# A fused top-k attention and SwiGLU kernel: each unit's product with V two turns after its top-k instead of four, with the exponential first in ScalarE's turn

## The chip, the cores and the metric

The kernel runs on one core of a Trainium2 chip. The metric is device microseconds of one execution. The kernel before takes 1840.27 us, the median of 3 runs (1840.24 to 1840.27).

A core has five engines, each with its own instruction stream that it works off in order: TensorE (PE in the profile; PEld is its weight load), VectorE (DVE), ScalarE (ACT), GpSimd (POOL) and SyncE (SP, which issues most DMAs here). An instruction that waits holds up everything behind it on its own engine, and nothing on the others until they need its result.

## The reference

Attention with a mask: per batch and head (8 batches, 8 heads, 576 tokens, head dimension 64), all but the 32 largest scores of a row are left out of the softmax. The result of the 8 heads side by side, 4608 tokens by 512, goes through a SwiGLU block with 1536 hidden columns. All is float32; the three weights arrive as float64.

```
scores = scale * np.matmul(q, k.transpose(0, 1, 3, 2))
kth = np.partition(scores, -top_k, axis=-1)[..., -top_k:-top_k + 1]
scores = np.where(scores >= kth, scores, -1000000000.0)
attn = np.exp(scores - np.max(scores, axis=-1, keepdims=True))
attn = attn / (np.sum(attn, axis=-1, keepdims=True) + 1e-09)
x = np.matmul(attn, v)        # then (B,H,S,D) -> (B*S, H*D)
g = x @ w_gate
out = (g / (1 + np.exp(-g)) * (x @ w_val)) @ w_out
```

## The kernel before

**Units and turns.** Attention is cut into 160 units (L281): a batch, a block of query rows, and a pair of heads. A batch has 20 units: 16 full ones (128 rows of each of two heads) and then 4 half ones (the last 64 rows of both heads, stacked into one tile of 128 partitions). The main loop (L718 to L774) has one turn per unit, and in turn n each engine works on a different unit:

- VectorE: `select(n)` (L326), the top-k of unit n: per head four MAX8 (L339) and three MATCH_REPLACE8 (L343), then a compare-and-multiply (L349) that leaves a penalty in `e`. Between these it does the rounding of the float64 weights (L124, L130) in the first turns, and one reciprocal (L382).
- TensorE: `scores(n+1)` (L304, L318), the transposes of a normalized unit (`turn`, L397), its product with V (`values`, L417, L426), transposes of new k and q (`prep`, L265, L273), and pieces of the feed-forward block.
- GpSimd: `penalize(n-1)` (L353): a bias (L359) and the sum e + scores (L361).
- ScalarE: `weigh(n-1)` (L364), the exponential with row sum (L370) and a small sum (L375); the scaling by the reciprocal (`normalize`, L385); and every copy out of PSUM: scores to `sc` (L309, L323), transposes to `et` (L398), attention output to `xT` (L441), k and q (L268 to L278), the feed-forward products (L505 to L507, L512) and sums (L593, L600, L624, L636).

The order on each engine is the order in which the Python code emits the instructions: the last lines (L781 to L794) chain every engine's instructions in that order. So where a call stands in the loop decides who waits for whom.

**How long a unit takes in turns.** Unit u has its top-k in turn u and its exponential in turn u+1. Its reciprocal and scaling come in turn u+2 (`over`, L721 and L724), its transposes at the head of turn u+3 (`TURN = 3`), and its product with V at the head of turn u+4 (`VALUES = 4`). The loop has four more turns than units. The tile `e` has 4 buffers.

**Feed-forward.** The attention output collects in `xT` blocks of 256 tokens by 512. When all of a block's units are in (`done`, L659), `feed(kb)` (L466) may run: 18 blocks. Per block, six times (s = 0 to 5) a gate product and a value product into a PSUM tile `f` (3 buffers). A gate product is followed by three ScalarE instructions (tanh, half, plus one) and a GpSimd product h * half; a value product by a ScalarE copy and a GpSimd product h * val. The tiles `half_g` and `val` share three buffers, tag "gv". Then comes the product with w_out, for block 0 directly (L526), for the others in seven partial products ("quarters", L566) whose operands and results GpSimd adds and subtracts (L573, L581, L586, L614, L552). `feed` is a generator; each step ("piece", cost 1) is 4 matmul instructions of 128x256, and 3 of a quarter's six matmuls cost 0.75. In the trace a matmul instruction on float32 shows as two records, so a piece is 8 records and a product (gate or value of one s) 16.

**How pieces are placed.** A turn's share of pieces is `share(n)` (L679): 6.4 per full unit (3.2 per half), less what the unit work of that turn costs TensorE. The turn's credit is spent at fixed places of the turn, `pieces(2)`, `pieces(1)`, `pieces(1)`, `pieces(6)`; in the last four units it is 8.

**Delayed work of ScalarE and GpSimd.** What follows a feed-forward product is not emitted at once, but put on the lists `on_act` and `on_pool`, which `flush` empties: both in `piece()` when they hold more than one entry, both at the turn's head, `on_act` after `pieces(2)`, `on_pool` after the scaling. A quarter adds flushes of its own. At the head of a turn the order is: `on_act`, `penalize(n-1)`, `on_pool`, transposes of n-3, product with V of n-4, scores of n+1 on TensorE, exponential of n-1, scores of n+1 out of PSUM.

The PSUM tiles of scores, transposes, av and kqps share 5 buffers (`ps_t`); `sc` has 2.

The lines of the code:

## Time and profile before

| | |
|---|---|
| median of 3 runs | 1840.27 us |
| the profiled execution, its own time | 1837.67 us |
| its span, first to last instruction | 1835.9 us |
| mean granted TensorE clock | 0.965 |
| PE busy | 1705.2 us (93%) |
| PEld busy | 1406.3 us (77%) |
| DVE busy | 1618.9 us (88%) |
| ACT busy | 1202.6 us (66%) |
| POOL busy | 1013.0 us (55%) |
| e + scores on GpSimd (L361), one of a full unit | 2.64 us |
| h * half and h * val on GpSimd (L508, L513), one | 1.28 us, 1.30 us |
| exponential of one head on ScalarE (L370) | 0.78 us |
| last threshold instruction of unit 159 (L349) ends at | 1737.5 us |

Busy time is the union of an engine's instructions, so waits are what is left. The chain that ended last is 83% PE. The 1.8 us between span and own time lie around the program; the median of the runs is 2.6 us above the profiled execution. In what follows a "turn n" of the trace runs from the end of unit n-1's last threshold instruction on VectorE (L349) to the end of unit n's.

### The profile page before, as it was taken

What the parts mean: (1) busy time and instruction counts of PE and PEld (TensorE: products, weight loads), DVE (VectorE), ACT (ScalarE), POOL (GpSimd) and SP (SyncE); (2) the same over time, 40 slices, a digit from 0 to 9 for tenths busy, and PEclk for the clock granted to TensorE, in tenths of its full rate; (3) what the DMA queues carried; (4) which work ended last, traced back from release to release, by engine and by line L of the source; (5) the groups of instructions that cost most, each with busy time, mean ns of one, the idle gap of its engine ahead of it and who ended that gap; (6) DMA issues with size and microseconds to landing.
All of it is one profiled execution on the core that took longest, in us unless ns stands there. A gap on an engine that the chain in (4) does not pass through costs nothing.

```text
span 1835.9 us, 30517 instructions
## 1 busy us (share of the span) xinstructions
PE 1705.2 (93%) x10756; PEld 1406.3 (77%) x10756; DVE 1618.9 (88%) x3405; ACT 1202.6 (66%) x2943; POOL 1013.0 (55%) x932
## 2 busy tenths in 40 slices
PE   3448999999999989999999999999999999999998
PEld 2336758777888878887888878888788878888887
DVE  7999999999999889997999989998999989998300
ACT  5667766677666667666767676767776766675431
POOL 3556746645555545655464646564556554646444
PEclk7668999999999999999999999999999999999999
DMA  7332121000200021000300012000300011000000
GB/s 189 98 84 91 59 66 26 12 1 21 73 1 12 2 66 27 12 1 15 73 19 1 12 42 52 1 12 2 74 19 12 1 36 32 1 12 12 1 13 12
DMA packets 109145, 59.65 MB, mean 32 GB/s; under 512 B 88512, under 2 KB 96704, under 8 KB 108992
## 3 DMA queue, kind: packets, MB, share of 16 engines
q1 hardware_dynamic: 107936, 57.44, 12.1%
q8 instruction: 85, 1.39, 0.3%
q14 instruction: 68, 0.56, 0.1%
q10 hardware_dynamic: 1056, 0.26, 0.1%
HBM read 48.23 MB, written 9.44 MB: 31 GB/s over the span
## 4 chain that ended last, share of the span: by engine, by line
PE 83%; DVE 3%; POOL 2%; ACT 2%; issue 2%; POOLq 0%; ACTq 0%
PE f L480 39%; PE x_ps L566 9%; PE av L426 8%; PE etps L397 7%; PE s L318 7%; PE y_ps L566 7%; PE s L304 2%; PE av L417 1%; DVE m L339 1%; PE kqps L273 1%; DVE rest L343 1%; PE o_ps L526 1%; POOL e L361 1%; POOL p L552 0%; ACT e L370 0%
## 5 line engine op out<-in xcount | busy, mean ns | idle before, releaser
L339 DVE MAX8 m<-rest 128x8 f32<-128x576 f32 x864 | 619.3, 758 | 2.2
L343 DVE MATCH_REPLACE8 rest<-m,rest 128x576 f32<-128x576 f32 x576 | 427.1, 754 | 0.0
L361 POOL TENSOR_TENSOR e<-e,sc 128x1152 f32<-128x1152 f32 (+1 forms) x160 | 382.7, 2392 | 79.7 <-DVE e L349 61.0
L480 PE MATMUL f<-xT,wg 128*128 128x256 f32 x1728 | 401.6, 382 | 0.0
L480 PE MATMUL f<-xT,wv 128*128 128x256 f32 x1728 | 400.4, 382 | 0.0
L480 PEld LDWEIGHTS f<-xT,wg 128*128 128x128 f32 x1728 | 323.0, 190 | 62.6 <-issue 21.0
L480 PEld LDWEIGHTS f<-xT,wv 128*128 128x128 f32 x1728 | 325.3, 190 | 59.5 <-issue 16.6
L508 POOL TENSOR_TENSOR h<-h,half_g 128x512 f32<-128x512 f32 x108 | 138.1, 1279 | 295.6 <-ACT h L507 295.1
L339 DVE MAX8 m<-sc 128x8 f32<-128x576 f32 x288 | 206.4, 757 | 105.8 <-ACT sc L309 57.9
L370 ACT ACTIVATE e<-e,bias 128x576 f32<-128x576 f32 x288 | 222.1, 777 | 89.5 <-POOL e L361 89.5
L397 PE MATMUL etps<-ident,e 128*128 128x128 f32 (+1 forms) x1312 | 184.0, 285 | 96.9 <-POOL size L120 40.8
L398 ACT COPY et<-etps 128x512 f32<-128x512 f32 (+1 forms) x448 | 184.4, 484 | 124.6 <-PE etps L397 123.6
L397 PEld LDWEIGHTS etps<-ident,e 128*128 128x128 f32 (+1 forms) x1312 | 158.3, 146 | 124.3 <-POOL size L120 43.3
L513 POOL TENSOR_TENSOR h<-h,val 128x512 f32<-128x512 f32 x108 | 139.9, 1295 | 186.0 <-ACT val L512 185.8
L385 ACT ACTIVATE e<-e,tot 128x576 f32<-128x576 f32 x288 | 211.9, 789 | 7.0 <-DVE tot L382 6.7
L343 DVE MATCH_REPLACE8 rest<-m,sc 128x576 f32<-128x576 f32 x288 | 213.0, 750 | 0.0
L318 PE MATMUL s<-kqT 64*128 64x288 f32 x1024 | 171.6, 445 | 5.8 <-ACT kqT L278 3.6
L349 DVE TENSOR_SCALAR e<-sc,m 128x576 f32<-128x576 f32 x288 | 171.8, 640 | 3.4
L426 PE MATMUL av<-et,v 128*64 128x128 f32 (+1 forms) x2560 | 172.4, 280 | 0.0
L323 ACT COPY sc<-s 128x288 f32<-128x288 f32 x512 | 163.9, 402 | 1.8 <-PE s L318 1.7
L426 PEld LDWEIGHTS av<-et,v 128*64 128x64 f32 x2560 | 135.7, 144 | 22.7 <-issue 6.6
L505 ACT ACTIVATE h<-f 128x512 f32<-128x512 f32 x108 | 65.3, 605 | 130.9 <-PE f L480 130.9
(71 smaller groups left out, 2010.0 us busy)
## 6 DMA issues: line engine op xcount, KB each, us to landing
v<-in_v_dram SPq DMA_DIRECT2D x32, 256.0 KB, 3.0
kq_in<-in_k_dram SPq DMA_DIRECT2D x63, 128.0 KB, 3.0
kq_in<-in_q_dram SPq DMA_DIRECT2D x63, 128.0 KB, 3.0
w<-in_moe_w_gate_dram SPq DMA_DIRECT2D x12, 512.0 KB, 3.7
w<-in_moe_w_val_dram SPq DMA_DIRECT2D x12, 512.0 KB, 3.8
w<-in_moe_w_out_dram SPq DMA_DIRECT2D x12, 512.0 KB, 3.6
out_dram<-o SPq DMA_DIRECT2D x40, 128.0 KB, 2.4
out_dram<-o SPq DMA_DIRECT2D x16, 256.0 KB, 2.4
```

What stands on the lines that cost most here:

```text
L318: nc.tensor.matmul(ps[:, 0:half], slab[d, q0 : q0 + P], slab[d, k0 : k0 + half])
L339: nc.vector.max(m[:, t, 8 * r : 8 * r + 8], cur[:, hs])
L343: nc.vector.match_replace(rest[:, hs], m[:, t, 8 * r : 8 * r + 8], cur[:, hs], LOWEST)
L349: nc.vector.tensor_scalar(e[:, hs], sc[:, hs], m[:, t, TOP_K - 1 : TOP_K], FAR, ALU.is_lt, ALU.mult)
L361: nc.gpsimd.tensor_tensor(e[:, every], e[:, every], sc[:, every], ALU.add)
L370: nc.scalar.activation(e[:, hs], e[:, hs], AF.Exp, bias=bias[:, t : t + 1], scale=scale, accum_out=tot[:, t : t + 1],)
L385: nc.scalar.mul(e[:, hs], e[:, hs], tot[:, t : t + 1])
L397: nc.tensor.transpose(ps[0:kl, c * P : (c + 1) * P], e[:, k0 : k0 + kl], ident[:])
L398: nc.scalar.copy(et[0:kl, c0 : c0 + cn, :], ps[0:kl, 0 : cn * P].rearrange("p (c j) -> p c j", c=cn),)
L426: nc.tensor.matmul(av[hh * R : (hh + 1) * R, 0:ql], v_last[:, hh, :] if c == J else vt[:, hh, c, :], moving, start=last and c == 0, stop=c ...
L480: nc.tensor.matmul(ps[:, i, :], w[:, kc, m * P : (m + 1) * P], x[:, kc, :], start=(kc == 0), stop=(kc == KC - 1),)
L566: nc.tensor.matmul(ps, lhsT, T[i][m], start=m == 0, stop=m == MQ - 1)
```

## The change

In the new order a unit has its exponential, reciprocal, scaling and transposes all in the turn after its top-k (the transposes late in it, in front of `pieces(6)`), and its product with V in the turn after that, behind the scores. The loop has two more turns than units, and `share` counts the unit work accordingly. At a turn's head ScalarE first gets the exponential, then the delayed feed-forward work, then the copies of the scores. GpSimd's delayed products are no longer emitted in `piece()` nor after the scaling, but at the head of the turn behind the sum e + scores. Where more than two wait when a "gv" buffer is wanted, the oldest are emitted then (the new function `gv`); the flushes of the quarters and at the start of a block remain.

```diff
+    def gv(name):
+        while len(on_pool) > 2:
+            on_pool.pop(0)()
+        return ffn.tile([P, 2, BLK], FP32, tag="gv", name=name, bufs=3)
...
-                half = ffn.tile([P, 2, BLK], FP32, tag="gv", name="half_g", bufs=3)
+                half = gv("half_g")
...
-                val = ffn.tile([P, 2, BLK], FP32, tag="gv", name="val", bufs=3)
+                val = gv("val")
...
-        if len(on_pool) > 1:
-            flush(on_pool)
...
-        for m, cost in ((n + 1, 0.7), (n - TURN, 0.6), (n - VALUES, 0.7)):
+        for m, cost in ((n + 1, 0.7), (n - 1, 0.6), (n - 2, 0.7)):
...
-    TURN, VALUES = 3, 4
-    for n in range(NU + VALUES):
+    for n in range(NU + 2):
...
-        over[n - 1] = normalize(n - 1) if 0 <= n - 1 < NU else no
-        norm = over.pop(n - 2, no)
+        norm = normalize(n - 1) if 0 <= n - 1 < NU else no
...
-        flush(on_act)
         if 0 <= n - 1 < NU:
             penalize(n - 1)
         flush(on_pool)
-        if 0 <= n - TURN < NU:
-            run(turn(n - TURN))
-        if n >= VALUES:
-            finish_unit(n - VALUES)
-        next(nxt, None)
         early[0]()
         if 0 <= n - 1 < NU:
             weigh(n - 1)
+        flush(on_act)
         run(nxt)
+        if n >= 2:
+            finish_unit(n - 2)
...
         dve(1)
         dve(1)
-        next(norm, None)
-        run(norm)
-        flush(on_pool)
         next(ahead, None)
         pieces(1)
         next(ahead, None)
         dve(1)
+        run(norm)
         pieces(1)
         dve(2)
         run(topk)
+        if 0 <= n - 1 < NU:
+            run(turn(n - 1))
         pieces(6)
```

More of the change, by code (lines that the diff above doesn't have):

```diff
@@ L714 @@
     no = iter(())
-    over = {}
-    TURN, VALUES = 3, 4
     due = [2.0]
-    for n in range(NU + VALUES):
+    for n in range(NU + 2):
         nh = n_heads(units[n][1]) if n < NU else 1
         topk = select(n) if n < NU else no
-        over[n - 1] = normalize(n - 1) if 0 <= n - 1 < NU else no
         nxt = scores(n + 1) if n + 1 < NU else no
         ahead = fetch(n + 2) if n + 2 < NU else no
-        norm = over.pop(n - 2, no)
+        norm = normalize(n - 1) if 0 <= n - 1 < NU else no
         def dve(k, beside=True):
```

## The prediction, written before the changed kernel ran

> **What bounds the kernel now.** I read the page's slices first, then windows of single stretches, then the timeline by engine around one change of feed-forward block, and last the waits. The slices say who is full where:

> ```profile
> PE   3448999999999989999999999999999999999998
> DVE  7999999999999889997999989998999989998300
> ACT  5667766677666667666767676767776766675431
> PEclk7668999999999999999999999999999999999999
> ```

> For four slices (184 us) DVE is full and PE is not; after that PE is full to the end, DVE has gaps, and in the last two slices DVE is done while PE works off feed-forward blocks. ACT is never full. So the time is PE's work plus PE's waits, and the waits lie at the start. The windows (columns: length, then busy time of PE, PEld, DVE, ACT, POOL, then PE's granted clock):

> ```profile
> 130.00:144.00 14.00, 7.40 (x45) 5.61 (x43) 13.50 (x30) 10.08 (x23) 8.20 (x9) 0.70 0.32 96
> 144.00:158.00 14.00, 6.81 (x41) 5.68 (x42) 14.00 (x29) 9.21 (x21) 7.81 (x7) 0.76 0.30 94
> 354.00:365.00 11.00, 6.74 (x42) 5.33 (x43) 10.99 (x25) 8.54 (x22) 4.24 (x4) 0.79 0.13 48
> 640.00:656.00 16.00, 11.38 (x80) 8.42 (x79) 6.60 (x13) 8.45 (x23) 9.39 (x12) 0.89 0.02 5
> 1012.00:1472.00 460.00, 456.72 (x2956) 380.22 (x2956) 436.84 (x919) 315.82 (x783) 258.42 (x234) 1.00 0.09 23
> ```

> The first two are turns 9 and 10, where PE idles half the time: no block is complete yet. The third is turn 29, idle again because block 2 is not complete. The fourth is one of the few stalls later on, and the last shows the rule: 99% busy. That this busy time is real I take from the spacing of weight loads: 16 of one product start at 1734.81 us and the next 16 at 1738.27 us, 0.216 us each, and it is the same all through the full stretch. One piece (8 records) is 1.73 us.

> The PE timeline at the start of block 2 gives the rest of the prices:

> ```profile
> 374.44 1.24 PE L318 MATMUL s<-kqT 64*128 64x288 f32 x8
> 375.62 3.72 PE L480 MATMUL f<-xT,wg 128*128 128x256 f32 x16
> ...
> 384.35 1.15 PE L397 MATMUL etps<-ident,e 128*128 128x128 f32 x9
> 385.33 0.39 PE L417 MATMUL av<-et,vlast 128*128 128x128 f32 x2
> 385.65 1.09 PE L426 MATMUL av<-et,v 128*64 128x128 f32 x16
> 386.68 1.24 PE L318 MATMUL s<-kqT 64*128 64x288 f32 x8
> 387.85 0.48 PE L480 MATMUL f<-xT,wg 128*128 128x256 f32 x1
> ```

> From start to start: transposes 0.98 us, product with V 1.35, scores 1.17, together 3.5 us a full unit. With the planner's 6.4 - 2.0 = 4.4 pieces, a full turn is 3.5 + 4.4 x 1.73 = 11.1 us of PE, against 10.56 us of DVE in the turns where DVE does not wait (thresholds of units 32 to 35, L349). PE is the longer one by 0.5 us, so it falls behind DVE until DVE waits for scores; that is the state of the full stretch.

> **Step 1, the feed-forward block starts two turns earlier.** In the new program order the first feed-forward matmul stands in turn 9 (24 matmul instructions) instead of turn 11, into PE idle time of 14.0 - 7.40 + 14.0 - 6.81 = 13.8 us. But the work then runs dry again: block 2 needs units up to 27, so PE waits for it in turn 31 now and in turn 29 then. It is cleaner to compare these two restarts. Now block 2 starts at 375.62 us. Then, turn 29 begins where DVE has finished unit 28, at 354.2 us (I take DVE's pace there as unchanged: it is full, and its instructions are the same in number). From there a chain is new, because xT's copy stands behind the exponential and the scores on ACT. The ACT timeline:

> ```profile
> 378.28 0.78 ACT L370 ACTIVATE e<-e,bias 128x576 f32<-128x576 f32 x1 [3.40 <-POOL e L361]
> ...
> 379.94 0.30 ACT L375 ACTIVATE tot<-tot,eps 128x2 f32<-128x2 f32 x1
> ```

> POOL's sum ends 2.8 us after DVE's threshold, the exponential takes 1.96 us (378.28 to 380.24), four copies of scores 1.28, two of xT 0.33: block 2 starts at 354.2 + 6.4 = 360.6. At 375.62 PE has by now done two scores and one transpose group more than then (2 x 1.17 + 0.98 = 3.3 us). PE comes out of a wait there, so 3.4 us run at half clock (the 640 window, after a wait of 4.6 us, has clock 0.89 over 16 us, about 3.5 us at half): 1.7 us lost. Gain: 375.6 - 360.6 - 3.3 - 1.7 = **10.0 us**. Bounds: 4 (VectorE delayed 3 us in turns 17 to 28, the clock lost twice) to 14.8 (xT's copy as early as now).

> **Step 2, the full stretch.** The units' work, the pieces and the copies are the same instructions; what changes is what PE can wait for. At the transposes (L397) PE now needs an e that was scaled in the same turn. With PE level with DVE, PE gets there at 1.17 + 1.35 + 4 x 1.73 = 9.4 us into the turn. On the other side: sum at 2.8, exponential to 4.7, scores and xT to 6.4, reciprocal after 10 of the 14 top-k instructions (about 6.8), then two scalings (1.47 us): 8.3. But ACT's feed-forward work stands ahead of the scalings: a gate is 0.605 + 0.601 + 0.641 = 1.85 us by its rows. With one gate it is 9.7 and the first scaling is out at 9.0, no wait; with a second gate left over from the turn before it is 10.8 for the first scaling, a wait of 1.4 us. If PE lags 2 us or more there is none, and PE lags by itself, 0.5 us more every full turn. Behind a waiting transpose stand up to six pieces and the next scores; behind the waiting exponential, ACT's copies, which PE needs for PSUM (3 buffers of f: two products waiting and one more to fill, 3.5 us, after 2.5 us of unit work; ACT is back by then). GpSimd's products, held back to the head, put one or two more of them (1.28 us each) between the first subtraction of a quarter and its addition: the third quarter would find its operand up to 2 us late at lag 0, and in time at lag 2.

> On the other side stand the stalls of now: 17 us of PE idle between 376 us and the tail. They come from POOL being stuck in feed-forward work when the sum is due:

> ```profile
> ACT e L370 <- POOL e L361: 89.5, 42, 4.9
> ```

> With the products at the head only, most of that cause goes; the quarters' own additions stay in front of the sum. Bounds for the stretch: -17 us (all stalls gone) to +103 full turns x 1.4 us = +144. I take **0**, near the low end, as PE has the longer turn and so the lag.

> **Step 3, the tail.** After the last scores there are 44.25 pieces against 52 now: these 7.75 pieces are the same two turns as step 1, not a second gain. Block 16 runs out sooner, so the last chain is open: exponential of unit 159 (behind the et copies of 158), reciprocal, output copy, scaling, transposes, et, V, xT. By the rows above: about 3.4 us of PE idle where now there are 1.0 + 0.4. **+2 us.**

> **Costed at nothing:** loads of v two turns earlier (DMA share 0.09); fewer or later flushes (order, no instruction); the smaller number of turns (empty ones). One weight piece moved ahead by a turn on DVE around turn 12, 1.2 us, made good in the next.

> **Sum.** 1835.9 - 10.0 + 0 + 2 = 1828 us of span; the own time 1.8 us more; the median of the runs 2.6 us above that: **1832 us**, 0.45% faster.

> [...]

> **Rivals.**
> - *The wait at the transposes (slower).* PE doesn't build up the lag, because DVE now waits for the exponential (L382 stands in DVE's stream, and its input hangs on ACT behind PE's last transposes): et copies 0.7, exponential 2.0 and a gate 1.85 must fit before 6.8, so DVE waits once the lag is above about 2.3 to 4 us. If it settles below 2, PE waits in most full turns. The gain is gone at 8 / 103 = 0.08 us a full turn. At 0.3 us: 1832 + 31 = 1863. For it: ACT has 8 of 11 us busy and now a serial chain; against it: PE is the longer one by 0.5 us a turn. Chance 0.26.
> - *Given back at the blocks (no change).* Each of 16 later blocks loses 0.5 us at its start (xT's copy late) or at the third quarter: 1840. Half of the blocks start a turn or more after they are complete, so these have cover. Chance 0.14.
> - *The present stalls vanish too.* 1832 - 10 to - 17: 1815 to 1822. Chance 0.08.
> - *The forecast*, 1822 to 1836: 0.52.

> That the change does not reach PE's order is excluded by the order itself: 24 matmuls in turn 9.

> Measurement tells 0.2% (3.7 us) from no change. Faster 0.60, same 0.14, slower 0.26. The range 1815 to 1862 takes in the bound of step 2 below and the slower rival up to its middle.

> **What would show it.** Right: feed-forward matmuls from about 131 us on, block 2 at about 361 us, PE 99% busy after 376 us, PE's wait at L397 a few us in all, the last threshold before 1737 us. Wrong: waits "PE etps L397 <- ACT e L385" of tens of us, clock windows of 0.5 all through the stretch, DVE waits at L382, or waits of L566 for POOL's additions.

## The result: 4.7% slower

The changed kernel takes **1926.99 us** (median of 4 runs, 1925.36 to 1929.49), the kernel before 1840.26 us beside it: ratio 1.0473, 95% interval 1.0455 to 1.0491. The forecast of 1832 and the range up to 1862 are both missed; the sign is wrong. The profiled execution has a span of 1927.7 us, against 1835.9 before: 91.8 us to explain.

The lines of the changed kernel's page that answer to those of before, one digit for each fortieth of the span:

```profile
PE   3459889798999989999999989999999999999988
...
DVE  7999889996999979998799977989897979998410
...
PEclk7669899899999999999999999999999999999989
```

PE still looks full, with 8s where 9s were. The clock row, all 9s from the fifth slice on before, now has 8s in the fifth, the eighth and the last but one, and DVE has more gaps. A digit hides a loss of 5%; the windows show it (length, then busy time of PE, PEld, DVE, ACT, POOL, PE's clock):

```profile
130.00:144.00 14.00, 12.24 (x62) 9.23 (x62) 11.60 (x26) 8.95 (x21) 6.54 (x7) 0.86 0.35 112
144.00:158.00 14.00, 14.00 (x83) 11.57 (x82) 14.00 (x31) 11.78 (x27) 9.55 (x9) 1.00 0.26 77
354.00:365.00 11.00, 5.74 (x36) 4.16 (x35) 11.00 (x25) 6.60 (x17) 3.88 (x4) 0.73 0.00 0
...
1012.00:1472.00 460.00, 437.78 (x2763) 356.26 (x2761) 402.28 (x856) 292.05 (x735) 244.22 (x226) 0.99 0.09 22
```

The first two rows show what was hoped for: PE is busy from 134 us on, because block 0 starts two turns earlier. In the third, PE idles and no block has started. The last is the full stretch: in the same 460 us PE is busy for 437.8 instead of 456.7 us and gets through 2763 matmuls instead of 2956, and DVE too does less (402 us of work instead of 437). Both engines wait more than before. Where, the waits say (in total us, times, longest):

```profile
DVE tot L382 <- ACT tot L375: 205.9, 71, 13.4
ACT e L370 <- POOL e L361: 203.0, 66, 7.9
...
PE etps L397 <- ACT e L385: 101.9, 33, 7.7
...
PEld o_ps L532 <- DVE wo L130: 12.6, 4, 4.1
```

Before, the same rows read 25.0 us (L382), 89.5 us (L370) and 10.9 us (L397). A row adds up all stages: of the 101.9 us at L397, 71.1 us lie before block 2 starts and 30.9 us between block 2 and block 17. (In `feed` the changed kernel's lines stand 6 lower: L486 is L480, L572 is L566.)

**Where the 91.8 us are.** I cut both traces at the first matmul of three feed-forward blocks:

| us | before | after | difference |
|---|---|---|---|
| first matmul of block 0 | 156.8 | 134.3 | -22.5 |
| first matmul of block 2 | 375.6 | 377.1 | +1.5 |
| block 2 to block 17 | 1393.1 | 1479.4 | +86.3 |
| block 17 to the end | 67.2 | 71.2 | +4.0 |

The early start of block 0 is there in full and gone by block 2. The loss is the full stretch. There I added, for each kind of matmul, the time from its start to the start of the next one on PE (a wait counts to the matmul ahead of it):

| us from block 2 to 17 | feed-forward products | quarters | transposes of e | V | scores | kq transposes | sum |
|---|---|---|---|---|---|---|---|
| before | 637.6 | 283.2 | 122.2 | 167.7 | 153.0 | 29.3 | 1393.1 |
| after | 652.0 | 305.2 | 135.1 | 180.0 | 157.6 | 49.5 | 1479.4 |

Of the 86.3 us, counting gaps of over 0.12 us beyond a matmul's own time, PE's waits rise from 22.9 to 82.1 us: 24.4 us in 12 waits between kq transposes and the transposes of e, 18.3 in 9 between a quarter and the transposes, 12.8 in 8 between a feed-forward product and the transposes. Time at half clock rises from 10.2 to 50.1 us; half of the 39.9 us, 20 us, is the most that it can have cost, as parts of these windows fall into the waits. 59 and 20 make 79. Unit work that block 2's start in an earlier turn has put behind it (16 scores and 9 transposes more, by 0.15 and 0.11 us) is 3.4 us of the rest.

**How such a wait comes about.** Two half-unit turns of the changed kernel, first ScalarE, then PE (start, length; in brackets the idle time ahead and what ended it):

```profile
1135.26 0.59 ACT L518 COPY val<-f 128x512 f32<-128x512 f32 x1 [3.38 <-PE f L486]
1135.74 0.78 ACT L385 ACTIVATE e<-e,tot 128x576 f32<-128x576 f32 x1
...
1142.59 0.58 ACT L278 COPY kqT<-kqps 128x512 f32<-128x512 f32 x1 [2.79 <-PE kqps L273]
...
1143.34 0.62 ACT L278 COPY kqT<-kqps 128x512 f32<-128x512 f32 x1
1143.81 0.81 ACT L385 ACTIVATE e<-e,tot 128x576 f32<-128x576 f32 x1
```

```profile
1131.50 3.72 PE L486 MATMUL f<-xT,wv 128*128 128x256 f32 x16
1136.57 0.77 PE L397 MATMUL etps<-ident,e 128*128 128x128 f32 x5 [1.35 <-ACT e L385]
...
1139.26 2.86 PE L572 MATMUL y_ps<-wo,h 128*128 128x256 f32 x12
1141.96 0.60 PE L273 MATMUL kqps<-ident,kq_in 128*128 128x128 f32 x4
...
1144.67 0.76 PE L397 MATMUL etps<-ident,e 128*128 128x128 f32 x5 [1.57 <-ACT e L385]
```

ScalarE is idle for 3.4 us with the scaling queued behind the copy of a product on which PE is still working. When PE ends it, ScalarE copies, scales, and only then PE may transpose. VectorE's reciprocal (L382) had ended at 1130.9 us, so it does not hold the scaling up. The scaling waits for PE, and PE for the scaling: a round trip within one turn. In the second turn the copies of kq do the same. ScalarE did not take the scaling ahead of the copy: the scaling had its input at 1130.9 us and started at 1135.74 us, behind the copy and its 3.38 us of idle time.

The other kind begins on GpSimd (the same kernel; POOL, ACT, PE):

```profile
455.42 0.73 POOL L558 TENSOR_TENSOR o<-p 128x256 f32<-128x256 f32 x1 [5.60 <-ACT p L599]
...
458.82 2.10 POOL L620 TENSOR_TENSOR h<-h,xT 128x256 f32<-128x256 f32 x3
460.87 0.22 POOL L359 TENSOR_SCALAR bias<-m 128x2 f32<-128x2 f32 x1
461.05 2.62 POOL L361 TENSOR_TENSOR e<-e,sc 128x1152 f32<-128x1152 f32 x1
```

```profile
463.70 0.77 ACT L370 ACTIVATE e<-e,bias 128x576 f32<-128x576 f32 x1 [7.87 <-POOL e L361]
...
466.60 1.48 ACT L385 ACTIVATE e<-e,tot 128x576 f32<-128x576 f32 x2
```

```profile
459.20 2.86 PE L572 MATMUL x_ps<-t,h 128*128 128x256 f32 x12
467.51 2.15 PE L397 MATMUL etps<-ident,e 128*128 128x128 f32 x9 [5.45 <-issue]
```

VectorE's threshold (L349) for this sum had ended at 453.6 us. GpSimd had then been idle for some time behind a copy of ScalarE that its next addition needs, and the sum (L361) stands behind that addition and the rest of the quarter's work: it ends 10 us after the threshold. The exponential stands behind the sum, the scaling behind the exponential, and PE idles 5.45 us. The nine transposes then take 2.15 instead of 1.15 us: the granted clock is 0.50 from 465.0 to 471.8 us. A sum this late is rare: over the 101 full units from unit 31 on, it ends 2.8 us after the threshold in the median, and more than 8 us after it in 9 of them.

### The profile page after: what moved, and what is told of

It is laid out like the page before. It is cut to its first block, busy times and chain, and to the rows that moved or that the text cites. A ratio compares the mean times of both kernels' runs of the same rounds, so it can differ in the third digit from the quotient of the medians.

```text
span 1927.7 us, 30528 instructions
## 1 busy us (share of the span) xinstructions
PE 1753.7 (91%) x10756; PEld 1408.1 (73%) x10756; DVE 1613.5 (84%) x3405; ACT 1192.8 (62%) x2943; POOL 1012.8 (53%) x932
## 4 chain that ended last, share of the span: by engine, by line
PE 70%; POOL 6%; DVE 5%; ACT 5%; issue 3%; POOLq 0%; ACTq 0%
PE f L486 34%; PE x_ps L572 7%; PE etps L397 7%; PE av L426 6%; PE s L318 6%; PE y_ps L572 5%; DVE m L339 2%; DVE rest L343 2%; PE av L417 2%; POOL e L361 2%; PE s L304 2%; ACT e L370 1%; POOL p L558 1%; ACT e L385 1%; POOL h L620 1%
## 5 line engine op out<-in xcount | busy, mean ns | idle before, releaser
L361 POOL TENSOR_TENSOR e<-e,sc 128x1152 f32<-128x1152 f32 (+1 forms) x160 | 382.5, 2390 | 533.7 <-DVE e L349 501.6
L486 PE MATMUL f<-xT,wg 128*128 128x256 f32 x1728 | 407.6, 385 | 2.7 <-ACT xT L441 2.7
L486 PE MATMUL f<-xT,wv 128*128 128x256 f32 x1728 | 404.8, 384 | 1.3 <-ACT half_g L512 1.3
L486 PEld LDWEIGHTS f<-xT,wg 128*128 128x128 f32 x1728 | 323.7, 192 | 52.9 <-issue 7.2
L486 PEld LDWEIGHTS f<-xT,wv 128*128 128x128 f32 x1728 | 323.5, 191 | 49.4 <-issue 6.2
L370 ACT ACTIVATE e<-e,bias 128x576 f32<-128x576 f32 x288 | 222.2, 778 | 203.2 <-POOL e L361 203.0
L397 PE MATMUL etps<-ident,e 128*128 128x128 f32 (+1 forms) x1312 | 191.9, 293 | 126.1 <-ACT e L385 101.9
L397 PEld LDWEIGHTS etps<-ident,e 128*128 128x128 f32 (+1 forms) x1312 | 162.2, 150 | 157.3 <-issue 57.1
L385 ACT ACTIVATE e<-e,tot 128x576 f32<-128x576 f32 x288 | 212.3, 791 | 16.5 <-DVE tot L382 16.5
L339 DVE MAX8 m<-sc 128x8 f32<-128x576 f32 x288 | 204.8, 747 | 10.2 <-ACT sc L323 9.2
L382 DVE RECIPROCAL tot<-tot 128x2 f32<-128x2 f32 (+1 forms) x160 | 25.0, 156 | 206.9 <-ACT tot L375 205.9
L318 PE MATMUL s<-kqT 64*128 64x288 f32 x1024 | 176.2, 464 | 2.7 <-ACT kqT L278 2.7
L323 ACT COPY sc<-s 128x288 f32<-128x288 f32 x512 | 166.0, 414 | 1.7 <-PE s L318 1.7
L426 PE MATMUL av<-et,v 128*64 128x128 f32 (+1 forms) x2560 | 165.4, 273 | 1.0 <-ACT et L398 1.0
L349 DVE TENSOR_SCALAR e<-sc,m 128x576 f32<-128x576 f32 x288 | 160.5, 594 | 3.5
L426 PEld LDWEIGHTS av<-et,v 128*64 128x64 f32 x2560 | 129.8, 140 | 31.3 <-issue 6.5
```

The costliest lines, as they stand in the source:

```text
L318: nc.tensor.matmul(ps[:, 0:half], slab[d, q0 : q0 + P], slab[d, k0 : k0 + half])
L323: nc.scalar.copy(sc[:, i * half : (i + 1) * half], ps[:, 0:half])
L339: nc.vector.max(m[:, t, 8 * r : 8 * r + 8], cur[:, hs])
L361: nc.gpsimd.tensor_tensor(e[:, every], e[:, every], sc[:, every], ALU.add)
L370: nc.scalar.activation(e[:, hs], e[:, hs], AF.Exp, bias=bias[:, t : t + 1], scale=scale, accum_out=tot[:, t : t + 1],)
L385: nc.scalar.mul(e[:, hs], e[:, hs], tot[:, t : t + 1])
```

## The experiments

**Theory A**: the loss comes from scaling and transposes in one turn. Rivals: the exponential first, or the reciprocal in the exponential's turn (VectorE's wait), or GpSimd's held-back products. Each ratio is to the kernel before, run beside it.

**GpSimd's products at the head only**, put into the kernel before:

```diff
-        if len(on_pool) > 1:
-            flush(on_pool)
...
+                half = gv("half_g")
...
         run(norm)
 
-        flush(on_pool)
```

> The order before, with one part of the change alone: GpSimd's feed-forward products only at the turn's head and through gv. Theory (the slowdown is the short way: exponential, reciprocal, scaling and transposes in one turn): within 10 us of 1840. Rival (GpSimd's products held back make the quarters and gv buffers late): most of the loss is here, 1880 or more, with PE waiting at L572 or ScalarE at L512/L518 for GpSimd.

1841.33 us, ratio 1.0007 [0.9997, 1.0016]. This part costs and gives nothing.

**The exponential first**, in the kernel before:

```diff
-        flush(on_act)
         if 0 <= n - 1 < NU:
             penalize(n - 1)
         flush(on_pool)
+        early[0]()
+        if 0 <= n - 1 < NU:
+            weigh(n - 1)
+        flush(on_act)
...
-        next(nxt, None)
-
-        early[0]()
-        if 0 <= n - 1 < NU:
-            weigh(n - 1)
         run(nxt)
```

> The order before, with the exponential of n-1 put first on ScalarE at the turn's head (ahead of on_act, of the et copies of n-3 and of xT's copy), nothing else. Theory: within 15 us of 1840, since with four turns nothing waits for that exponential in the same turn. Rival (ScalarE stuck behind GpSimd's sum at the head holds up PE's PSUM buffers): 1880 or more, with PE idle at the head of turns.

2229.83 us, ratio 1.2127 [1.2107, 1.2147]. My expectation fell by far; the rival held. Its waits:

```profile
ACT e L370 <- POOL e L361: 531.9, 144, 8.4
...
DVE m L339 <- ACT sc L323: 295.8, 90, 10.6
PE s L318 <- ACT et L398: 233.8, 107, 7.2
```

The copies of et now stand behind the exponential, which stands behind GpSimd's sum; the scores on PE wait for the copies of et, and the top-k for the scores. So ScalarE's order alone can cost 21% (with PE at half clock for 214 us between block 2 and block 17), though ScalarE is busy for only 66% of the span in the kernel before. In the changed kernel the transposes and their copies stand at the end of the turn, not behind the exponential, and it has no row of scores waiting for copies of et. So this loss is not the changed kernel's; that the two share the mechanism, a copy that stands behind a wait in ScalarE's order, is argued.

**Three turns with the transposes late, or the scaling and the transposes late.** Both are the changed kernel with the transposes and V a turn later (the loop and `share` accordingly):

```diff
-        if n >= 2:
-            finish_unit(n - 2)
+        if n >= 3:
+            finish_unit(n - 3)
...
-        if 0 <= n - 1 < NU:
-            run(turn(n - 1))
+        if 0 <= n - 2 < NU:
+            run(turn(n - 2))
```

and the second also with `norm = normalize(n - 2)`: reciprocal and scaling a turn later, so again in the turn of the transposes.

> The changed kernel with the transposes and the product with V each a turn later (three turns in all); exponential, reciprocal and scaling still in one turn. Theory: the wait of PE at the transposes goes (102 us of L397 behind L385 in the changed kernel, under 20 here), and most of the 87 us with it: 1840 to 1870, though VectorE still waits at L382 for some 100 us or more. Rivals (GpSimd's or ScalarE's order): 1900 or more.

1884.18 us, 1.0234 [1.0218, 1.0251], between the two expectations.

> As the kernel before in this list (three turns), but the reciprocal and scaling are a turn later too, so that scaling and transposes fall in one turn and the exponential in the turn before. It tells the two waits apart. If PE's wait for the scaling in the same turn is the cause, 1880 or more with L397 waiting; if it is VectorE's wait for the exponential in the same turn (L382, 206 us in the changed kernel), 1830 to 1860 with L382 under 30 us.

1918.89 us, 1.0440 [1.0419, 1.0462]. The pair tells the two waits apart. In the first DVE still waits 158.1 us at L382, PE's waits in the stretch are 36.9 us and half clock 10.2 us. In the second the wait at L382 is gone (21.5 us), and PE's waits are nearly as bad as in the changed kernel: 75.7 us, half clock 44.8 us. **So PE's waits come with scaling and transposes in one turn, not with the reciprocal's wait.** Taken apart, they save 43 of the 87 us; that is half of it, and Theory A said most. The first run still loses 36.9 us between block 2 and block 17. Its waits are 14 us more than before; by the spacing of matmuls it loses 20 us behind the transposes, 11 behind the scores and 8 behind V, and what causes these is open.

**The reciprocal left out** agrees with it. The changed kernel, scaling by a constant, so that the output is not normalized:

```diff
-        nc.vector.reciprocal(tot[:, 0:nh], tot[:, 0:nh])
...
-            nc.scalar.mul(e[:, hs], e[:, hs], tot[:, t : t + 1])
+            nc.scalar.mul(e[:, hs], e[:, hs], eps[:])
```

> The changed kernel without the reciprocal: e is scaled by a constant tile, so VectorE no longer waits for the exponential's sum; exponential, scaling, transposes and all else stay in their places (the softmax is not normalized, so the output is another one). If VectorE's wait at L382 (206 us) is what costs, 1850 to 1880; if it is ScalarE's chain from exponential to scaling to PE's transposes and back, 1905 to 1930, with L397 waiting for L385 as before.

1922.67 us, 1.0457 [1.0443, 1.0471]: taking away VectorE's largest wait, 205.9 us, gave 4 us. PE's waits stay (84 us between block 2 and block 17, 82 with the reciprocal), and VectorE now waits 181.3 us in all for ScalarE's copies of the scores (L323 and L309, 9.2 and 1.0 us in the changed kernel).

**Which copies hold the scaling up: those of kq.** The changed kernel with the kq transposes and copies of the turn behind the scaling:

```diff
-        next(ahead, None)
         pieces(1)
-        next(ahead, None)
         dve(1)
         run(norm)
+        next(ahead, None)
         pieces(1)
+        next(ahead, None)
```

> The changed kernel, with the transposes of new k and q and their copies on ScalarE placed behind the scaling instead of ahead of it. In the trace of the changed kernel PE waits 24 us between kqps and the unit's transposes, in 12 places. Theory (ScalarE's queue ahead of the scaling sets the wait): this pair's wait under 8 us and 15 to 25 us faster than the changed kernel, about 1905. Rival (another wait takes its place in the same turns): within 8 us of 1927.

1902.78 us, 1.0339 [1.0323, 1.0355]: 24 us less, and the waits between kq transposes and transposes of e fall from 24.4 to 6.0 us. So the place of the kq transposes and copies was worth 24 us: 20 between block 2 and block 17, and 4 by an earlier start of block 2.

**Three turns from the kernel before.** The old head, the reciprocal and scaling in the exponential's turn (`TURN, VALUES = 2, 3`); then this with GpSimd's products at the head; then the first of them with kq behind the scaling as above:

> The order before, with the reciprocal and scaling moved into the turn of the exponential (late in it), the transposes one turn and the product with V one turn earlier (three turns in all), and everything at the turn's head left as it was: transposes and V ahead of the scores, ScalarE's et copies ahead of the exponential. Theory (the harm is what stands around the late transposes: PE's scores right behind them need PSUM that ScalarE frees behind its wait for GpSimd's sum): 1825 to 1845, since a turn less brings 7 us of PE idle at the start. Rival (exponential and reciprocal in one turn are enough to make VectorE wait, 158 us in the run with late transposes, and that costs time): 1870 or more.

1884.85 us, 1.0233 [1.0207, 1.0258]. The theory fell, and the rival's time came; its cause is tested below.

> As the kernel before in this list, with GpSimd's products only at the turn's head too. Then the sum e + scores is not behind feed-forward products and VectorE's wait at L382 should be shorter. Theory: equal to that kernel or up to 10 us faster. Rival (GpSimd's deferral costs once the way is shorter): 10 us slower or more.

1881.39 us, 1.0209 [1.0175, 1.0243]: 3.5 us less, within the scatter of its runs (1869.95 to 1882.65). GpSimd's held-back products cost nothing here either.

> The three-turn order with the old head (1884.85), with the transposes and copies of new k and q behind the scaling. In that run PE waited 25 us between kqps and the next transposes, with 34 us more of half clock than before. Theory (the loss there is the scaling that stands behind the k and q copies on ScalarE): 1840 to 1860. Rival (VectorE's wait at L382, 160 us there, is what costs): 1875 or more.

1856.40 us, 1.0092 [1.0078, 1.0106]. The scaling's place in its turn is worth 28 us here too, even with the transposes at the next head, and the theory held. DVE still waits 130.4 us at L382, so that wait was not what cost these 28 us; 17 us against the kernel before are left.

**Two trials at the early stretch.** More rounding of weights on VectorE ahead of block 0 (`5 / 11` to `7 / 11`), since block 2 starts no earlier than before:

> The changed kernel, with the weights' rounding paced at 7/11 instead of 5/11 of VectorE's top-k steps, so that the last weights are ready before block 0 asks for them. In the changed kernel turn 14 takes 22.7 us because the rounding is called from inside the product with w_out. Theory: block 2 starts 8 to 15 us before 377 us and the kernel ends as much earlier, 1912 to 1920. Rival (VectorE's early turns grow by the same rounding): within 4 us of 1927.

1933.89 us, 1.0505 [1.0486, 1.0524]. Block 0 starts at 148.3 and block 2 at 380.2 us. It fell: work moved ahead on a full VectorE delays the units as much.

**V behind the first two pieces**, in the turn of the transposes in the kernel before (`VALUES = 3`), and in the changed kernel:

```diff
-        if n >= VALUES:
-            finish_unit(n - VALUES)
         next(nxt, None)
...
         pieces(2)
+        if n >= VALUES:
+            finish_unit(n - VALUES)
         flush(on_act)
```

> The order before, with only the product with V a turn earlier (in the turn of its transposes, behind pieces(2)): three turns from top-k to V in place of four, and neither the exponential nor the scaling moved. Theory (a shorter way pays where no wait enters a turn): block 0 starts one turn earlier, about 7 us of PE idle filled, 1830 to 1838. Rival (the product with V now waits for the et copies, or xT's copy comes late): 1845 or more.

1916.20 us, 1.0413 [1.0399, 1.0428]. The theory fell, the rival held.

> The changed kernel with the product with V two pieces later in its turn, so that two pieces stand between the scores and V and the et copies have time. In the run with late transposes PE lost some 30 us in short waits from transposes to scores to V (PSUM and et copies). If these count in the changed kernel too, 1895 to 1915; if the wait for the scaling takes all of it, within 8 us of 1927.

1936.46 us, 1.0526 [1.0512, 1.0541], slower than either expectation. Both are slower than the kernel that they change: xT's copy on ScalarE now waits for PE's two pieces (the first of the two kernels):

```profile
ACT xT L441 <- PE av L426: 240.9, 124, 5.3
```

It is 74.0 us before; in the second kernel the row is 245.6 us, against 13.3 in the changed kernel. So it is a round trip of the same kind with another copy; that the whole loss comes from it is argued.

**GpSimd's late sum.** What was left open was how much of the waits begins there. The sum is put into GpSimd's queue as soon as the unit's top-k is issued, ahead of the last pieces and their additions:

```diff
-        if 0 <= n - 1 < NU:
-            penalize(n - 1)
...
         run(topk)
+        if n < NU:
+            penalize(n)
```

First in the changed kernel with kq behind the scaling, then in the kernel before, then in the three-turn kernel of 1856.4 us:

> The changed kernel with the kq transposes behind the scaling, and GpSimd's sum of a unit put into its queue as soon as the unit's top-k is issued (ahead of the last pieces of the turn and their quarter additions) instead of at the next turn's head. Theory (the rest of the waits at the transposes comes from GpSimd's sum standing behind quarter additions): the wait of the exponential for the sum falls from some 200 us to under 80 us, the waits of PE for f->T and v->T in the stretch fall by more than half, time 1875 to 1888 against 1902.8 for the kernel without this step. Rival (the sum is late only because VectorE's threshold is late, and the additions now wait behind it): the quarters' matmuls wait for the additions instead, time 1898 to 1912.

1866.09 us, 1.0142 [1.0126, 1.0157], 37 us less than without it and less than either expectation. The wait of the exponential for the sum falls from 203.9 to 110.1 us (under 80 was expected), the waits between quarters and transposes from 17.5 us to under 0.5, half clock from 37.4 to 8.7 us.

> The kernel before with this one step: GpSimd's sum put into its queue right behind the unit's top-k. Theory: before's own 23 us of PE waits in the stretch come in part from the late sum (4.8 us at 640 to 656 us alone), so the time falls by 4 to 10 us, to 1830 to 1836. Rival: quarter additions stuck behind the waiting sum cost as much as they gave, 1838 to 1846.

**1832.86 us, 0.9961 [0.9948, 0.9975]**: this beats both kernels. Before's stall in the window from 640 to 656 us shows why (POOL, first the kernel before, then this one):

```profile
641.64 2.08 POOL L614 TENSOR_TENSOR h<-h,xT 128x256 f32<-128x256 f32 x3
...
643.87 2.61 POOL L361 TENSOR_TENSOR e<-e,sc 128x1152 f32<-128x1152 f32 x1
```

```profile
637.37 2.63 POOL L361 TENSOR_TENSOR e<-e,sc 128x1152 f32<-128x1152 f32 x1
...
643.58 2.10 POOL L614 TENSOR_TENSOR h<-h,xT 128x256 f32<-128x256 f32 x3
```

The sum comes 6.5 us earlier and the additions 1.9 us later. PE is busy there for 15.99 of 16 us, against 11.38:

```profile
640.00:656.00 16.00, 15.99 (x128) 12.48 (x128) 11.90 (x24) 11.84 (x31) 9.68 (x13) 1.00 0.02 6
```

From block 2 to 17 it takes 1386.6 us instead of 1393.1; PE's waits fall by 4.9 us (one wait of 4.8 is gone) and half clock by 3.4.

> The three-turn kernel with kq behind the scaling (1856.4) and the early sum. Theory: exponential and scaling come earlier, PE's waits of 36 us in the stretch fall to about 20, time 1838 to 1848. Rival: no change by the sum, 1853 to 1860, and what is left is VectorE's wait at the reciprocal (130 us).

1840.85 us, 1.0005 [0.9996, 1.0014]. With both steps, one turn less costs nothing against the kernel before, though DVE still waits 114.0 us at L382; but the sum early without the turn less gains 7 us.

**The scaling right behind the exponential.** The kernel without the reciprocal again (not normalized), `run(norm)` moved up to stand behind `weigh(n - 1)`, ahead of every copy:

> The changed kernel without the reciprocal (output not normalized), the scaling by a constant standing right behind the exponential, so that no copy of a feed-forward product, of kq or of scores stands ahead of it on ScalarE. Theory (the scaling is late because of the copies ahead of it): PE's waits at the transposes fall from 84 us in the stretch to under 25 us (what remains is GpSimd's late sum), half-clock time falls from 52 us to under 25, time 1845 to 1860 against 1922.7 with the same constant at its old place. Rival (the chain of sum, exponential, scaling, transposes in one turn is too long by itself): the waits stay over 50 us, time 1895 to 1920.

1895.36 us, 1.0298 [1.0284, 1.0312]: 27 us less than with the scaling at its old place, so the theory's time fell. The waits of PE at the transposes (behind quarters, V, kq and feed-forward) do fall, from 58 us with the scaling at its old place to 15; the larger ones left, 13.4 us behind quarters, all follow an exponential that waited for the sum. But PE's other waits rise in their place: between feed-forward products 12 us (9 with the scaling at its old place), from the transposes to the scores 9.9; all waits come to 56.9 us, against 84. The rival's total was right, but not its place. Here the exponential waits 223.9 us in all for GpSimd's sum, and the feed-forward copies stand behind it. I read this as follows, without a run that shows it: with the sum as late as it is, ScalarE's order can only choose who waits.

## Why the prediction was wrong

- **Step 2 is the step that failed**: "I take 0, near the low end, as PE has the longer turn and so the lag." It came out at +86.3 us, inside the bounds of -17 to +144. The turn in which I worked it out was a full one. All 12 waits behind kq lie in turns of half units, which have less of VectorE's work to cover the round trip from PE through a copy and the scaling back to PE (that this is why is argued); and the large ones behind quarters lie in turns with a late sum. I had put the sum's end at 2.8 us after the threshold, from one turn in which GpSimd was idle; over the full units from unit 31 on, the kernel before already had 5.2 us in the median and up to 12.3. In the row above it is 10 us, because "the quarters' own additions stay in front of the sum" was named but not priced. The two steps that answer these, kq behind the scaling and the sum early, take 24 and 37 us off the time.
- **The lag is no cushion** (argued from the two timelines and the kq runs). The prediction let PE fall behind VectorE until the transposes need not wait. ScalarE's queue ties them: its copies wait for PE's products, so a PE that lags makes the scaling late by the same amount. The scaling was priced with gates in front that cost their 1.85 us of work; the wait of the copy for its product, 3.38 us in the row shown, was left out.
- **Step 1**: block 0 starts at 134.3 us (about 131 said), block 2 at 377.1 instead of 360.6 us. The term that fell is "I take DVE's pace there as unchanged": unit 28's threshold ends at 373.5 instead of 354.2 us. By unit 15 it is 9.9 us late. Most of that comes in turn 14, which takes 22.7 instead of 16.0 us: block 0's product with w_out comes two turns earlier and calls for its weights at once, so the rounding of weights falls into that turn (the wait at L532 above). The other 9.4 us come from unit 15 to 28, where DVE waits 16.3 us at L382; without the reciprocal, block 2 starts at 369.6 us. So block 2 starts 1.5 us later, not 15.0 us earlier. The restart chain itself, 6.4 us from the threshold to xT, was priced well: PE starts on the block a little before, and the fourth matmul (records 7 and 8) waits for xT's last copy until 379.65 us, 6.1 us after the threshold (the changed kernel, PE):

```profile
377.05 1.56 PE L486 MATMUL f<-xT,wg 128*128 128x256 f32 x6
379.65 0.70 PE L486 MATMUL f<-xT,wg 128*128 128x256 f32 x2 [1.03 <-ACT xT L441]
```

- **Step 3**: +2 us said; from block 17 to the end it is +4.0 us.
- **The rivals.** The slower one, with a chance of 0.26, named the right place: PE waits at the transposes in the same turn. Its reason failed: it put the wait down to VectorE's wait at L382, and without the reciprocal PE's waits stay. It priced 0.3 us in each full turn, 31 us; the waits are fewer and far larger, and those behind kq lie in half-unit turns. "The present stalls vanish too" failed, as GpSimd's products were not what cost the time: without them in the way, the kernel before is the same (ratio 1.0007), and the exponential's wait for the sum falls only from 89.5 to 84.1 us; with the additions moved behind the sum it gains 7 us.
- **The clock.** Of the signs named for "wrong", waits of tens of us at L397, waits at L382 and windows of half clock all came. By the traces, half clock is at most 20 of the 86 us.

Open: the two-turn kernel with both steps (1866.1 us) is still 24 us longer than the kernel before from block 2 to 17 (1417.5 against 1393.1), and its waits of over 0.12 us are only 8 us more (30.9 against 22.9). By the spacing of matmuls the 24 us lie behind feed-forward products, transposes and V, about 10 us each, less 6 behind quarters and scores; what causes the part that is not such waits is open. What the feed-forward copies alone cost, with the sum early, was not tried.

## What to carry to other kernels

Before two dependent steps are moved into one turn, follow the chain through every engine's queue that it crosses, and count for each instruction ahead in those queues not its length but when its own input comes: a copy that waits for PE (3.38 us in the row shown) in front of a result that PE waits for is a round trip. Work it out in the shortest turn and in the one with the most foreign work in the queue, not in the average one. Where one engine's late result starts such a chain, as GpSimd's sum here, put that instruction ahead of work that can wait; this was worth 7 us in the kernel before and 37 us in the one with the short chain.

## What the runs showed of the hardware

In these two traces the falls go with how little PE works in one cell of that grid. I added up its work per cell from block 2 to block 17, each matmul at its usual spacing and waits left out; this is an estimate. With one exception (a cell of 1.62 us, in the changed kernel), the clock went from full to half after just those cells that hold at most 1.16 us of work, 14 in the two traces; all other cells at full clock hold at least 1.33 us. The wait at 1127.6 us lies across the border of two cells and leaves 1.33 us of work in the first and 2.6 in the second. In the kernel before, the window at 1507.2 us followed two waits of only 0.92 and 0.89 us: both lie in one cell, with 1.09 us of work.

A wait's total says little of its price: taking away 205.9 us of VectorE's waits at L382 gave 4 us of the time, and of PE's 101.9 us at L397 70% lie before block 2, where the changed kernel is only 1.5 us behind.
